# Hidden layer of the late units by sixteen block products for eighteen, and the decay's sigmoid by the hyperbolic tangent

## The chip, the cores and the metric

The kernel runs on one core of one Trainium2 chip. The metric is the device time of the whole kernel in microseconds (us). The engines are named as in the profile: PE (TensorE matmuls), PEld (its weight loads), DVE (VectorE), ACT (ScalarE), POOL (GpSimd), SP (the queue from which most transfers are issued).

## The reference

A gated recurrence (4 batches, 8 heads, 768 steps, head size 48) is followed by a two-layer block with the quick gelu. All data is float32.

```python
f = 1.0 / (1.0 + np.exp(-f_logit))
for t in range(S):
    state = f[:, :, t, :, None] * state + np.einsum('bhd,bhe->bhde', k[:, :, t], v[:, :, t])
    y[:, :, t] = np.einsum('bhd,bhde->bhe', q[:, :, t], state)
x = y.transpose(0, 2, 1, 3).reshape(B * S, H * D)      # 3072 tokens x 384
h = x @ w_in                                           # 384 x 2048
g = h * (1.0 / (1.0 + np.exp(-1.702 * h)))
out = g @ w_out                                        # 2048 x 384
```

## The kernel before, in words

The 3072 tokens are cut into 12 units of 256 tokens (`U`), three per batch. For each unit `attention(n)` computes y in a form without a loop over time: six levels of scores (`level`, `levels`), products of decays made on POOL (`begin_gates`, tile `tot`), states per chunk of 64 tokens (`st`), and y from masked scores and states. `begin_f` turns the gate's logits into the layout of the kernel and takes their sigmoid into tile `F`; for the late units DVE turns (L332) and ACT takes the sigmoid of 128x1024 in place (L337). The last part of a unit writes y through `yT` into `xT` (`to_x`, DMAs from SP), which holds the 384 columns in three thirds of 128 by 256 tokens; the last unit has one token more, since a unit's outputs are shifted by one token.

The two-layer block works on `xT`. `w_in` and `w_out` stay in SBUF. The 2048 hidden columns are 16 blocks of 128 (`ff`). `mlp_h` computes one block of h at a time: three matmuls with 256 moving columns (tokens) into one PSUM bank, and a gelu by ACT into a tile `g` (L785, L789). Units 0 to 2 are done in pieces while weights still arrive (`mlp_block`: `mlp_h` and `mlp_o`). From unit 3 on (`mlp_unit`) all 16 blocks of h are done and then the output by `mlp_o7`, which already uses seven products of half-size blocks for eight: 2x2 blocks of tokens (128) by 192 output columns, with sums of g (`sums_of_a`, `last_sum`, on DVE) and of `w_out` (`sums_of_b`, once) and sums of the results on the way out (`p1` to `p7`, `store`).

PE's order is written out by hand. `merge(n, ...)` emits the attention parts of one unit and puts pieces of the block's work from the list `fill` between them, by a share of columns for each kind of part (`late`); so unit n - 1's h and out products stand between unit n's attention parts. `xT` of unit n - 1 is made at the head of merge n. The other engines' instructions are placed by a scheduler. PSUM has eight banks: four single ones with the tag `mm` that rotate over h, out and turned blocks, two for scores (`sc`) and two for y.

For every fp32 matmul in the code the profile shows two records.

Of the kernel before, what the change touches and what calls it, by code (L numbers as in the profile page):

```python
# [23 lines left out]
def kernel(  # L24
# [37 lines left out]
    P = 128  # L62
# [37 lines left out]
    A = const.tile([P, 2 * NP, 2, HS], F32, name="A")  # L100

    def keep_up(times, columns=384, of=None):

        if times:
            pt = ps.tile([P, columns], F32, tag="mm", name=f"idle_{next(serial)}", bufs=4)
        for _ in range(times):
            lhs, rhs = of or (ident, masks.rearrange("p l f t -> p (l f t)"))
            nc.tensor.matmul(pt, lhsT=lhs, rhs=rhs, start=True, stop=True)  # L108
# [169 lines left out]
    def load_v(n):  # L278


        if n >= NALL:
            return
        b, s0 = n // NU, n % NU * U
        vts[n] = ld.tile([P, 2, DM], F32, tag="vt", name=f"vt_{n}", bufs=2)
        vrs[n] = ld.tile([P, DM], F32, tag="vr", name=f"vr_{n}", bufs=2)
        nc.sync.dma_start(
            out=vts[n][:, 1].rearrange("p (h d) -> p h d", h=H), in_=v[b, :, s0:s0 + HALF, :].rearrange("h p d -> p h d")
        )
        for i in range(4):
            t0 = s0 + U - 32 * (i + 1)  # L290
            nc.sync.dma_start(
                out=vrs[n][32 * i:32 * (i + 1)].rearrange("p (h d) -> p h d", h=H),
                in_=v[b, :, t0:t0 + 32, :].rearrange("h p d -> p h d"),
            )
# [11 lines left out]
    def attention(n):  # L306
# [19 lines left out]
        def turn(j, outs, fn=None):  # L326

            if n >= N_FILL:
                for f in (1, 0):
                    out = outs(f)  # L330
                    at, step = (0, 1) if f else (HALF - 1, -1)
                    nc.vector.transpose(  # L332
                        view(out, at, [[HALF, NP], [step, R4], [R4 * step, 32]]),
                        by_half[:, j, f].rearrange("p a (j d) -> p (a j) d", j=R4)[:, :, :32],
                    )
                if fn:
                    nc.scalar.activation(F, F, fn)  # L337
                return
            for j0 in range(0, R, 4):
                pt = ps.tile([P, 4, P], F32, tag="mm", name=f"t_{n}_{j}_{j0}", bufs=4)  # L340
# [6 lines left out]
                for f in (1, 0):  # L347
                    at, step = (j0, 1) if f else (HALF - 1 - j0, -1)
                    nc.scalar.activation(
                        view(outs(f), at, [[HALF, NP], [R * step, 16], [step, 4]]),  # L350
                        pt.rearrange("p j (a f i) -> p f a i j", a=NP, f=2)[:, 1 - f],
                        fn if fn and n < N_FILL - 1 else AF.Copy,
                    )
            if fn and n == N_FILL - 1:
                nc.scalar.activation(F, F, fn)

        def begin_f():
            turn(0, lambda f: F[:, ORDER.index(f) * SLOT:(ORDER.index(f) + 1) * SLOT], AF.Sigmoid)
            if n >= N_FILL or (n == 1 and 0 == 0):
                load_raw(n + 1, 0)  # L360
# [164 lines left out]
        def turn_k(a0):  # L525
            if a0 == 0:
                new_kn()
            pt = ps.tile([P, 2, 2, P], F32, tag="mm", name=f"tkn_{n}_{a0}", bufs=4)
# [70 lines left out]
        def _():  # L599
# [21 lines left out]
            xT = xTs[n] = mlp.tile([P, NK, width(n)], F32, tag="xT", name=f"xT_{n}", bufs=3)  # L621
            for f in (1, 0):
# [6 lines left out]
            if n == NALL - 1:  # L629

                pl = ps.tile([P, NP], F32, tag="mm", name="y_last", bufs=4)
# [10 lines left out]
                to_x(lambda h: (yl[rows(h), :NK], lambda r, d: yl[r:r + d, NK]), xT[:, :, U:], 1)  # L642
# [48 lines left out]
    def sums_of_a(n, g, b):  # L691

        j = b % 2
        t0, t1 = slice(0, G), slice(G, 2 * G)
        tt = nc.vector.tensor_tensor
        if b < 2:
            g["S", j] = mlp.tile([P, FG, width(n)], F32, tag="g", name=f"S_{n}_{j}", bufs=6)
            tt(g["S", j][:, :, t1], g[j][:, :, t0], g[j][:, :, t1], ALU.subtract)
        else:
            tt(g[j][:, :, t1], g[j][:, :, t1], g[j + 2][:, :, t1], ALU.add)  # L700
            tt(g["S", j][:, :, t0], g[j][:, :, t1], g[j][:, :, t0], ALU.subtract)

    def last_sum(n, g):

        for j in range(2):
            by = slice(0, G)
            nc.vector.tensor_tensor(g[j + 2][:, :, by], g[j + 2][:, :, by], g["S", j][:, :, by], ALU.subtract)

    def mlp_o7(n, g):
        a = lambda i, j: lambda f: g[j * 2 + f // FG][:, f % FG, i * G:(i + 1) * G]  # L710
        s = lambda i: lambda f: g["S", f // FG][:, f % FG, i * G:(i + 1) * G]
        b = lambda i, j: lambda f: quarter(w_out, i, j)[:, f]
        T_ = lambda i: lambda f: T[i][:, f] if i < 4 else T[4](f)
        t = {}

        def out_(tt):
            if "o" not in g:
                g["o"] = mlp.tile([P, U // P, DM], F32, tag="osb", name=f"osb_{n}", bufs=1)
            return g["o"][:, tt]

        def row(name):
            t[name] = mlp.tile([P, HC], F32, tag=name, name=f"{name}_{n}", bufs=1)
            return t[name]

        def p1():
            nc.scalar.copy(row("p1"), t["X"])

        def p4():
            nc.scalar.copy(row("p4"), t["W"])

        def p2():
            nc.scalar.copy(out_(0)[:, :HC], t["X"])
            last_sum(n, g)

        def p6():
            nc.scalar.copy(row("p6"), t["Y"])

        def p5():
            nc.scalar.copy(row("p5"), t["Z"])

        def p7():
            nc.vector.tensor_tensor(row("u3"), t["p1"], t["Y"], ALU.add)
            nc.vector.tensor_tensor(out_(1)[:, :HC], t["u3"], t["p4"], ALU.subtract)
            nc.vector.tensor_tensor(out_(1)[:, HC:], t["u3"], t["p5"], ALU.add)
            store(n, 1, out_(1))

        def p3():
            nc.vector.tensor_tensor(out_(0)[:, HC:], t["p1"], t["Z"], ALU.add)
            nc.vector.tensor_tensor(out_(0)[:, HC:], out_(0)[:, HC:], t["p6"], ALU.add)
            store(n, 0, out_(0))  # L750


        products = (
            ("X", a(0, 0), b(0, 0), p1, True), ("W", a(1, 1), T_(4), p4, True), ("X", a(0, 1), b(1, 0), p2, False),
            ("Y", s(0), T_(2), p6, True), ("Z", a(1, 0), T_(1), p5, True), ("Y", s(1), T_(3), p7, False),
            ("Z", a(0, 1), b(1, 1), p3, False),
        )

        def one(bank, lhs, rhs, done, new, f):
            if new and f == 0:  # L760
                t[bank] = ps.tile([P, HC], F32, tag="mm", name=f"o_{n}_{bank}", bufs=4)
            nc.tensor.matmul(  # L762
                t[bank], lhsT=lhs(f), rhs=rhs(f), start=(new and f == 0), stop=(f == HF - 1), skip_group_check=True,
            )
            if f == HF - 1:
                done()
        return [(HC, lambda p=p, f=f: one(*p, f), 0) for p in products for f in range(HF)]


    xTs = {}  # L770

    def width(n):

        return U + (n == NALL - 1)

    def mlp_h(n, ffs, g, sums=False):
        t = {}

        def one(ff, c):
            if c == 0:  # L780
                if ff % FG == 0:
                    g[ff // FG] = mlp.tile([P, FG, width(n)], F32, tag="g", name=f"g_{n}_{ff}", bufs=6)
                t["ph"] = ps.tile([P, width(n)], F32, tag="mm", name=f"h_{n}_{ff}", bufs=4)
# [4 lines left out]
            if c == NK - 1:  # L788
                nc.scalar.activation(g[ff // FG][:, ff % FG, :], ph, AF.Gelu_apprx_sigmoid)  # L789
                if sums and ff % FG == FG - 1:  # L790
                    sums_of_a(n, g, ff // FG)
                if width(n) > U:

                    by = g[ff // FG][:, ff % FG, U:]
                    if ff == 0:
                        g["last"] = mlp.tile([P, 1, DM], F32, tag="sum", name="sum_last", bufs=3)
                        nc.vector.tensor_scalar(g["last"][:, 0], w_out[:, 0, :], by, None, op0=ALU.mult)
                    else:
                        nc.vector.scalar_tensor_tensor(
                            g["last"][:, 0], w_out[:, ff, :], by, g["last"][:, 0], op0=ALU.mult, op1=ALU.add  # L800
                        )
        return [(NK * U, lambda ff=ff: [one(ff, c) for c in range(NK)], ff // FG * NPC + ff % FG + 1) for ff in ffs]

    def mlp_o(n, ffs, g, done):
# [3 lines left out]
        def one(tt, ff):  # L808
            if ff == ffs[0]:
                t["po"] = ps.tile([P, DM], F32, tag="mm", name=f"o_{n}_{tt}_{ff}", bufs=4)  # L810
# [13 lines left out]
    def mlp_unit(n):  # L824
        g = {}

        def last_token():
            po = ps.tile([P, DM], F32, tag="mm", name="o_last", bufs=4)
# [4 lines left out]
        if width(n) > U:  # L833
            o.insert(3 * HF, (DM, last_token, 0))
        return mlp_h(n, range(NFF), g, True) + o
# [72 lines left out]
    def merge(n, fill, columns, share, pieces=0, hold=0, by=1.0, chores=(), deal=()):  # L908
# [9 lines left out]
        for kind, fn in parts:  # L918
            ready = state["done"]
            fn()  # L920
            for chore in chores[:2]:
                chore()
            chores = chores[2:]
# [27 lines left out]
    UNIT = NFF * NK * U + U // P * NFF * DM  # L951

# [24 lines left out]
    for n in range(3, NALL):  # L977
        fill += mlp_unit(n)
    with nc.allow_non_contiguous_dma("one token"):
        for h in range(2):  # L980
            nc.sync.dma_start(out=q_end[h * HS:h * HS + D], in_=q[B - 1, h::2, S - 1, :].rearrange("a d -> d a"))
    for n in range(4, NALL):
        merge(n, fill, NFF * NK * U + 7 * HF * HC, late, chores=list(sums_of_b()) if n == 4 else ())
# [31 lines left out]
```

## Time and profile before

| | |
|---|---|
| time, median of 3 runs | 628.38 us (627.27 to 629.58) |
| span of the profiled execution | 627.9 us |
| PE, PEld, DVE, ACT, POOL busy | 602.8, 517.5, 385.8, 260.3, 39.9 us |
| h matmuls, L785 | 1152 records, 257.4 us busy |
| gelu of h, L789 | 192, mean 383 ns |
| out products by seven, L762 | 1008 records |
| DVE sums of g, L698, L700, L701, L707 | 18 each, mean 685 to 692 ns |
| POOL products of decays, L383, by size of output: 512, 256, 128 columns | 12 each, mean 1039, 693, 479 ns |
| ACT table loads, L337 and L789 | 9 and 10, 1283 ns each |

In the rows of the profile, a group is a line of the kernel, an engine, an operation, and output and input tiles with their shapes; "x" is the number of records. The mean of a matmul is the time from its start to its end in the pipeline; the next one starts earlier, so the pace is read from starts. Unit 4's h begins at 264 us, and later units follow every 46 us.

### The profile page before, as it was taken

Reading aid. Unit: us, or ns where it says so; the run is one execution under the profiler, and the core shown is the slowest. Engines: PE = TensorE matmul, PEld = TensorE weight load, DVE = VectorE, ACT = ScalarE, POOL = GpSimd, SP = SyncE. Lnnn points to the kernel's source line nnn. Section 1 sums busy time; section 2 is a strip of 40 time slices with the busy share of each in tenths; the row PEclk is TensorE's granted clock in tenths of the full one; section 3 lists DMA queues with packets and bytes.
Section 4 is the critical chain, followed back from the end, with each engine's and each line's share of the span. In section 5 each row is a group of like instructions: output and inputs, shape, how many; then the busy total and the mean of one; then the engine's idle time right before and its main releaser. Section 6 shows DMA issues by size and latency. Waiting matters only on the chain.

```text
span 627.9 us, 17094 instructions
## 1 busy us (share of the span) xinstructions
PE 602.8 (96%) x7314; PEld 517.5 (82%) x7314; DVE 385.8 (61%) x632; ACT 260.3 (41%) x544; POOL 39.9 (6%) x91
## 2 busy tenths in 40 slices
PE   7958999889999999999999999999999999999997
PEld 5647776757678688989989989989989889889896
DVE  1778976575876755677566577656658645521441
ACT  3436543533244534543544454354354353233220
POOL 3010030020001001001001001001001001000000
PEclk9898999989999999999999999999999999999999
DMA  7646675652034444444452342552161121001000
GB/s 171 183 126 165 170 161 158 148 139 76 2 92 99 122 100 105 105 94 110 122 135 60 76 109 73 142 123 68 45 160 33 44 59 27 27 1 27 26 1 25
DMA packets 83308, 58.20 MB, mean 93 GB/s; under 512 B 33633, under 2 KB 75265, under 8 KB 83233
## 3 DMA queue, kind: packets, MB, share of 16 engines
q1 hardware_dynamic: 82192, 55.55, 35.4%
q10 hardware_dynamic: 1041, 1.57, 1.0%
q8 instruction: 57, 0.93, 0.7%
q14 instruction: 18, 0.15, 0.1%
HBM read 43.98 MB, written 8.39 MB: 83 GB/s over the span
## 4 chain that ended last, share of the span: by engine, by line
PE 87%; DVE 6%; ACT 3%; DMA 2%; issue 1%; SPq 1%; ACTq 0%; DVEq 0%
PE h L785 38%; PE o_X L762 8%; PE o_Y L762 8%; PE o L811 8%; PE o_Z L762 7%; PE sc L392 6%; PE o_W L762 4%; PE t L344 3%; PE y L616 2%; PE sc L576 2%; PE y L488 1%; PE idle L108 1%; DVE a L221 1%; DMA xT<-yT 1%; ACT yT L627 1%
## 5 line engine op out<-in xcount | busy, mean ns | idle before, releaser
L785 PE MATMUL h<-xT,w_in 128*128 128x256 f32 (+1 forms) x1152 | 257.4, 381 | 2.4 <-ACT g L789 1.9
L785 PEld LDWEIGHTS h<-xT,w_in 128*128 128x128 f32 x1152 | 216.4, 190 | 34.2 <-ACT g L789 2.1
L789 ACT ACTIVATE g<-h 128x256 f32<-128x256 f32 (+1 forms) x192 | 72.0, 383 | 156.8 <-PE h L785 156.5
L477 DVE TENSOR_TENSOR X<-X,tot 128x1024 f32<-128x1024 f32 x45 | 55.1, 1224 | 62.6 <-PE sc L392 49.4
L448 ACT COPY Kc<-X 128x512 f32<-128x512 f32 x72 | 48.0, 666 | 83.4 <-DVE X L477 51.3
L811 PE MATMUL o<-w_out,g 128*128 128x384 f32 x192 | 67.5, 501 | 3.0 <-DVE w_out L222 3.0
L811 PEld LDWEIGHTS o<-w_out,g 128*128 128x128 f32 x192 | 36.2, 194 | 26.0 <-DVE w_out L222 3.6
L762 PE MATMUL o_X<-w_out,g 128*128 128x192 f32 x288 | 52.6, 331 | 0.0
L762 PE MATMUL o_Y<-T,S 128*128 128x192 f32 x288 | 51.9, 329 | 0.0
L441 DVE COPY_PREDICATED A<-masks,sc 128x256 f32<-128x256 uint32 (+1 forms) x108 | 50.9, 534 | 0.1
L762 PEld LDWEIGHTS o_Y<-T,S 128*128 128x128 f32 x288 | 46.9, 190 | 1.5 <-issue 0.7
L762 PEld LDWEIGHTS o_X<-w_out,g 128*128 128x128 f32 x288 | 46.7, 190 | 1.0
L383 POOL TENSOR_TENSOR tot<-F 128x512 f32<-128x512 f32 x12 | 12.5, 1039 | 478.2 <-DVE st L594 429.3
L392 PE MATMUL sc<-X,Kc 48*64 48x64 f32 x1440 | 31.1, 224 | 10.7 <-ACT Kc L448 9.6
L392 PEld LDWEIGHTS sc<-X,Kc 48*64 48x64 f32 x1440 | 26.4, 138 | 18.0 <-ACT Kc L448 11.4
L332 DVE STREAM_TRANSPOSE X<-raw 128x512 f32<-128x512 f32 x36 | 37.9, 1101 | 2.9 <-PE y L616 2.8
L700 DVE TENSOR_TENSOR g<-g,g 128x512 f32<-128x512 f32 x18 | 12.5, 692 | 40.4 <-ACT g L789 40.4
L627 ACT COPY yT<-y 48x256 f32<-48x256 f32 x92 | 33.7, 366 | 7.8 <-PE y L616 5.3
L473 DVE TENSOR_TENSOR X<-X,tot 128x512 f32<-128x512 f32 x30 | 20.3, 688 | 13.1 <-PE sc L392 11.0
L383 POOL TENSOR_TENSOR tot<-tot 128x256 f32<-128x256 f32 (+4 forms) x60 | 24.6, 410 | 4.7
L762 PE MATMUL o_W<-T,g 128*128 128x192 f32 x144 | 24.9, 326 | 0.0
L762 PE MATMUL o_Z<-w_out,g 128*128 128x192 f32 x144 | 24.9, 326 | 0.0
(92 smaller groups left out, 629.1 us busy)
## 6 DMA issues: line engine op xcount, KB each, us to landing
bits<-in_moe_w_out_dram SPq DMA_DIRECT2D x8, 768.0 KB, 5.0
raw<-in_f_logit_dram SPq DMA_DIRECT2D x48, 96.0 KB, 2.3
raw<-in_k_dram SPq DMA_DIRECT2D x48, 96.0 KB, 2.3
raw<-in_q_dram SPq DMA_DIRECT2D x44, 96.0 KB, 2.3
bits<-in_moe_w_in_dram SPq DMA_DIRECT2D x7, 576.0 KB, 6.2
k_tok<-z SPq DMA_DIRECT2D x56, 64.0 KB, 1.8
kt<-k_tok SPq DMA_DIRECT2D x14, 256.0 KB, 2.8
out_dram<-osb SPq DMA_DIRECT2D x18, 192.0 KB, 1.8
```

Of the source, the lines that this page charges most:

```text
L332: nc.vector.transpose(view(out, at, [[HALF, NP], [step, R4], [R4 * step, 32]]), by_half[:, j, f].rearrange("p a (j d) -> p (a j) d", j=R4) ...
L383: nc.gpsimd.tensor_tensor(tn, t2[:, :, 0], t2[:, :, 1], ALU.mult)
L392: nc.tensor.matmul(t["sc"][g * HS:(g + 1) * HS, h, a, s, :], lhsT=t["Kc", l][rows(h), x:x + HS], rhs=rhs(h, a, g), start=True, stop=True,)
L441: nc.vector.copy_predicated(out=view(A, at, dims), mask=mask.bitcast(U32), data=got)
L448: nc.scalar.copy(c.rearrange("p (n two m) -> p n two m", two=2, m=m), view(X, KF * SLOT, [[2 * m, SLOT // (2 * m)], [(KR - KF) * SLOT + m, ...
L473: nc.vector.tensor_tensor(x, x, y, ALU.mult)
L477: nc.vector.tensor_tensor(x, x, y, ALU.mult)
L627: copy(view(yT[rows(h)], at, [[U, NP], [step, HS]]), py[columns(h, g), g, :, f, :])
L762: nc.tensor.matmul(t[bank], lhsT=lhs(f), rhs=rhs(f), start=(new and f == 0), stop=(f == HF - 1), skip_group_check=True,)
L785: nc.tensor.matmul(ph, lhsT=w_in[:, c, ff * P:(ff + 1) * P], rhs=xTs[n][:, c, :], start=(c == 0), stop=(c == NK - 1))
L789: nc.scalar.activation(g[ff // FG][:, ff % FG, :], ph, AF.Gelu_apprx_sigmoid)
L811: nc.tensor.matmul(t["po"], lhsT=g[ff // FG][:, ff % FG, tt * P:(tt + 1) * P], rhs=w_out[:, ff, :], start=(ff == ffs[0]), stop=(ff == ffs[ ...
```

## The change

For units 4 to 11 a new `mlp_h16` takes the place of `mlp_h`. The first twelve blocks of the hidden columns are seen as three rows of four blocks, `w_in` as a matrix of 3 by 3 parts (row of hidden columns by a third of the 384 inputs), and the tokens as two halves, so h of the three rows is a 3x3 by 3x2 product of blocks. Done block by block it is 18 block products; here it is 16, each of a sum of `w_in` parts and a sum of x parts, each over four blocks of hidden columns with 128 moving columns. The products are put in four chains; in a chain each product adds to what stands in the bank, and most running sums on the way are one summand of an output and are read out before the chain goes on. An output needs one or two such summands: the first is copied by ACT, the second added by DVE, then ACT takes the gelu in place; one output is complete at once and goes through the gelu from the bank. The last four blocks of hidden columns are computed as before, one at a time, between the chains' products, in the order `SEQUENCE`.

The sums of `w_in` are made once: those in new tiles by `sums_of_w` (POOL and DVE, as chores of merge 4, now three to a part), those that overwrite `w_in` by `sums_in_place` in the middle of unit 3's out products. The sums of x (`sums_of_x`) are eleven POOL instructions per unit, right after `xT` is made. `g` becomes three tiles of eight blocks for six of four; `xT` and two tiles of sums share three buffers; the four single PSUM banks are named one by one (`bank`, `lanes`). `sums_of_a` comes after all of h. Two of the intermediate rows of the out part are summed in the output tile. In the last unit (one token more) the halves have 129 columns, the chains run over two blocks at a time, and the row sums of the last token come after h. The decay's sigmoid becomes 0.5 + 0.5 tanh(x/2) from unit 1 on, with the affine part on POOL (`half_up`).

```diff
@@ turn, begin_f @@
-                        fn if fn and n < N_FILL - 1 else AF.Copy,
+                        (AF.Tanh if n else AF.Sigmoid) if fn else AF.Copy, scale=0.5 if fn and n else 1.0,
...
+        def half_up():
+            nc.gpsimd.tensor_scalar(F, F, 0.5, 0.5, op0=ALU.mult, op1=ALU.add)
+        def sigmoid():
+            nc.scalar.activation(F, F, AF.Tanh, scale=0.5)
+            half_up()
@@ load_v, turn_k @@
-        vrs[n] = ld.tile([P, DM], F32, tag="vr", name=f"vr_{n}", bufs=2)
+        vrs[n] = ld.tile([P, DM], F32, tag="vr", name=f"vr_{n}", bufs=1)
...
+            if n < N_FILL + 1:
+                pt = bank([P, 2, 2, P], f"tkn_{n}_{a0}")
+            else:
+                pt = ps.tile([P, 2, 2, P], F32, tag="sc", name=f"tkn_{n}_{a0}")
@@ end of attention @@
+            if width(n) > U:
+                nc.gpsimd.memset(xT[:, :, U + 1:], 0.0)
...
+            if n > N_FILL:
+                sums_of_x(n)
@@ sums_of_a, last_sum @@
+        S = g["S"] = g_tile(f"S_{n}", width(n))
+        fs = [slice(f, f + HF // 2) for f in (0, HF // 2)]
+        for f in fs:
+            tt(S[:, f, t1], g[0][:, f, t0], g[0][:, f, t1], ALU.subtract)
+        for f in fs:
+            tt(g[0][:, f, t1], g[0][:, f, t1], g[1][:, f, t1], ALU.add)
+        for f in fs:
+            tt(S[:, f, t0], g[0][:, f, t1], g[0][:, f, t0], ALU.subtract)
@@ mlp_o7 @@
         def p2():
-            nc.scalar.copy(out_(0)[:, :HC], t["X"])
+            plus(0, left, "X")
             last_sum(n, g)
...
         def p7():
-            nc.vector.tensor_tensor(row("u3"), t["p1"], t["Y"], ALU.add)
-            nc.vector.tensor_tensor(out_(1)[:, :HC], t["u3"], t["p4"], ALU.subtract)
-            nc.vector.tensor_tensor(out_(1)[:, HC:], t["u3"], t["p5"], ALU.add)
-            store(n, 1, out_(1))
+            plus(1, left, "Y")
+            plus(1, right, "Y")
+            store(n, 1, g["o"][:, 1])
@@ new @@
+    CHAINS = (
+        (("D5", "b21", 3), ("N6", "E12", 2), ("C4", "E4", 4), ("N3", "E15", 0), ("a00", "E6", 1), ("N4", "E10", 5)),
+        (("N5", "b21", None), ("N1", "b11", 1), ("D11", "E11", None), ("D8", "E3", 0)),
+        (("a22", "E3", None), ("D9", "E9", 4), ("N7", "b10", None), ("N2", "E14", 2)),
+        (("a10", "E0", None), ("D2", "b11", 3)),
+    )
+    NEGATIVE = 0, 2, 5
+    SEQUENCE = "0 1 2 0 1 2 p 0 1 2 p 0 1 2 p 0 3 3 p 0".split()
+    LANE = {"0": 0, "1": 1, "2": 2, "3": 1, "p": 3}
...
+        by("E4", "b10", sub, "b00")
+        by("E12", "E4", add, "b21")
+        by("E3", "b20", add, "b21")
+        by("E10", "b01", add, "b21")
+        by("E0", "E10", sub, "b11")
+        by("E15", "E12", add, "b11")
+        by("E6", "E10", sub, "E15")
+        by("E9", "b00", sub, "b21")
+        by("E11", "b10", add, "b11")
+        by("E11", "E11", add, "E3")
+        by("E14", "E4", sub, "b20")
...
+            for t in range(group.start, group.stop):
+                nc.tensor.matmul(
+                    ph[:, t - group.start], lhsT=WA[a][:, t * P:(t + 1) * P], rhs=E[n][b],
+                    start=(i == 0 and t == group.start), stop=(i == len(CHAINS[chain]) - 1), skip_group_check=True,
+                )
+            if out is None:
+                return
...
+            if out == CHAINS[0][-1][2]:
+                nc.scalar.activation(to, ph, AF.Gelu_apprx_sigmoid, scale=scale)
+            elif (group.start, out) not in begun:
+                begun.add((group.start, out))
+                nc.scalar.copy(to, ph)
+            else:
+                nc.vector.tensor_tensor(to, to, ph, ALU.add)
+                nc.scalar.activation(to, to, AF.Gelu_apprx_sigmoid, scale=scale)
...
+        def end():
+            sums_of_a(n, g)
+            if width(n) > U:
+                sum_last(g)
@@ mlp_unit @@
-            o.insert(3 * HF, (DM, last_token, 0))
-        return mlp_h(n, range(NFF), g, True) + o
+            o.insert(6 * HF, (DM, last_token, 0))
+        if n > N_FILL:
+            return mlp_h16(n, g) + o
...
+        return mlp_h(n, range(NFF), by_block) + [(0, end, 0)] + o[:4 * HF] + [(0, sums_in_place, 0)] + o[4 * HF:]
@@ merges @@
+    H16 = 16 * FG * G + FG * NK * U
...
-        merge(n, fill, NFF * NK * U + 7 * HF * HC, late, chores=list(sums_of_b()) if n == 4 else ())
+        merge(n, fill, (H16 if n > N_FILL + 1 else NFF * NK * U) + 7 * HF * HC, late, chores=w_sums if n == 4 else [])
```

## The prediction

> **What bounds the kernel now.** I read the page's busy shares and its clock row first, then the busy times by stage, then the waits of the stage that changes, and last the timeline, because the mean duration of a matmul is a latency and not its pace.
>
> ```profile
> PE 602.8 (96%) x7314; PEld 517.5 (82%) x7314; DVE 385.8 (61%) x632; ACT 260.3 (41%) x544; POOL 39.9 (6%) x91
> ...
> PEclk9898999989999999999999999999999999999999
> ...
> 286.20:332.20 46.00, 46.00 (x593) 42.01 (x592) 29.26 (x46) 21.15 (x44) 2.81 (x6) 1.00 0.44 109
> 332.20:378.10 45.90, 45.90 (x597) 42.12 (x597) 29.71 (x47) 20.97 (x43) 2.81 (x6) 1.00 0.35 84
> 378.10:423.90 45.80, 45.80 (x594) 42.05 (x593) 29.61 (x47) 21.02 (x43) 2.81 (x6) 1.00 0.47 114
> ```
>
> The last three lines are one unit each (stretch, length, then busy PE, PEld, DVE, ACT, POOL). From unit 4 on PE is busy all of it at full clock, with DVE at 29.5 us, ACT at 21 and POOL at 2.8 of 45.8 us. PE's largest waits between 264 and 605 us are these, in total, times and longest:
>
> ```profile
> PEld sc L392 <- issue: 3.7, 13, 0.3
> PEld y L488 <- issue: 2.3, 7, 0.3
> PEld y L616 <- issue: 1.3, 6, 0.2
> PEld o_Y L762 <- ACT p L736: 0.3, 1, 0.3
> PEld y L616 <- DVE F L332: 0.2, 1, 0.2
> ```
>
> Only the last two, 0.5 us, are for another engine: the order written out for PE is the bound, and a column taken off PE is worth its pace. The pace, from start to start:
>
> ```profile
> 380.02 2.87 PE L762 MATMUL o_X<-w_out,g 128*128 128x192 f32 x16
> 382.72 2.76 PE L762 MATMUL o_W<-T,g 128*128 128x192 f32 x16
> 385.32 1.46 PE L762 MATMUL o_X<-w_out,g 128*128 128x192 f32 x8
> ...
> 550.99 0.60 PE L532 MATMUL tkn<-ident,X 128*128 128x128 f32 x4
> 551.19 0.38 ACT L789 ACTIVATE g<-h 128x256 f32<-128x256 f32 x1 [0.91 <-PE h L785]
> 551.32 0.30 PEld L785 LDWEIGHTS h<-xT,w_in 128*128 128x128 f32 x2
> 551.43 0.38 PE L785 MATMUL h<-xT,w_in 128*128 128x256 f32 x1
> ```
>
> The 16 o_W records take 385.32 - 382.72 = 2.60 us, 162.5 ns each at 192 columns. By the same reading of the trace's starts, h records of 256 columns come every 216 ns (217 to 218 over a unit), o records of 384 every 322, and the four 128-column records at 550.99 every 0.11 us. Every fp32 matmul in the code is two records: 16 blocks by 3 make 48 matmuls, and a unit has 96 h records.
>
> **What the skill says.** (1) The Trainium skill, "TensorE: Matmul & The Clock Gate", "Back-to-back issue gap", gives N/2.4 + 2.5 ns warm. The trace agrees if a record streams each column twice: 2 x 192/2.4 + 2.5 = 162.5, 2 x 256/2.4 + 2.5 = 215.8. For 128 columns that is an estimate of 109.2 ns. (2) The same page, "LDWEIGHTS (loading the stationary operand)", has P/1.2 ns: 107 for 128 weight columns, so weight load and matmul would be just level. Trace: weight loads of 64 columns last 136 ns, of 128 columns 190, so 54 ns per 64, which agrees; and the first two loads of the filler at 39.61 us start 0.11 us apart. The same section on the gap also says that a stream of N=128 pairs ran at 81 ns where the formula has 56; doubled that would be 162. No run here shows such a stream of plain 128-column matmuls; the four at 550.99 are transposes, whose weight loads last 141 ns and not 190. (3) "ScalarE: Activation LUTs", "What ACT_TABLE_LOAD costs": 1283 ns; the trace has exactly 1283, twice per late unit (L337 and L789). It lists tanh beside sigmoid; whether the set of the gelu used here holds it, it doesn't say. (4) "GPSIMD Engine Reference", "1. Specifications": POOL shares its SBUF interface with DVE. The trace agrees: the five small POOL products of a unit take 2.09 us alone and 3.46 and 4.02 us where DVE is converting weights.
>
> **The change, part by part.**
>
> *h of units 4 to 11.* It removes 12 blocks x 3 = 36 matmuls of 256 columns, 72 records: 72 x 216 = 15.55 us. It adds 16 products x 4 blocks = 64 matmuls of 128 columns, 128 records: 128 x 109.2 = 13.98 us. Four plain blocks stay. That is 1.57 us per unit; unit 11 (258 for 257 columns, halves of 129 at 110 ns) gets 1.5. Eight units: -12.5 us. Bounds of the pace: 107 (the load alone) and 162.
>
> *Evictions of h.* 12 ACT gelus of 383 ns (4.6 us) become 5 ACT copies of a 128x512 bank (L533: 591 ns), 6 gelus of the same size (about 650) and 5 DVE adds (L700: 692): ACT 6.9 us, DVE +3.5. ACT comes to about 23 and DVE to 33 of 44 us: neither becomes the bound. What counts is that a chain's bank is read between its products, and PE may not write on. Reading costs about 0.2 us to start (the gelus start 0.2 us after a block's end), 0.6 to 0.7 for the instruction and about 0.1 back: 1.0 us. A product is 8 x 109 = 0.87 us, a plain block 6 x 216 = 1.3 us, so the hand-written sequence puts 1.7 us ahead of chain 0's second product and 3.0 us ahead of each later one. Alone, nothing waits. But both engines take their queues in order, and DVE is full from 359.9 to 370 us with transposes of 1.1 us in the middle of h: an add that stands behind two of them is late by some tenths. I take 0.2 us per unit (bounds 0 and 1.5): +1.6 us.
>
> *Sums of x.* 11 POOL sums of 128x128. Nearest row: L383 with 128x128, 479 ns; 11 make 5.3 us. They start when xT has landed: its last DMA is issued until 395.06 us and lands in 1.8 to 2.6 us, so about 397.2; h begins at 401.79 in the old trace. Since merge 5 still emits the old number of columns for a shorter unit, the stock of out products ahead of h shrinks by 1,024 columns, 1.7 us, to about 400.1. The first sum needed, the third, is there at 398.7, wanted by the third product at 401.8; the eighth at 401.1, wanted after 405. Hidden, with 3 us to spare. xT, two sum tiles and g now turn over each unit, but what they overwrite was last read by h or out products that PE had done by then. Cost 0, up to 4 us per unit if the price is three times as high.
>
> *Sums of h and the out part.* The eight DVE sums of 0.69 us stay eight, but six now come after h: 4.2 us from about 1 us behind its end, while PE first has 2.0 us of attention and three products of 2.6. Hidden; the states (L594, L595) behind them on DVE have 4 us before the y products want them. One DVE op and one copy fewer per unit. 0.
>
> *Weight sums.* 9 POOL and 2 DVE instructions of about 1.04 us in merge 4, DVE at 61% there: hidden. The seven in-place sums (5 DVE, 2 POOL, some 0.7 to 1.0 us each) come in unit 3's out part, with 8 to 9 us before unit 4's h; the first product wants one of them at once. +0.7 us (0 to 2.5).
>
> *Decay by the tangent.* It takes away up to 19 table loads of ACT and adds a POOL pass over 128x1024 for units 1 on, about 1.7 us by the slope of L383's rows. In a late unit F is ready at 388.5 and first used at 370 of the next unit, 27 us on: nothing either way. In units 1 and 2 a table load or POOL pass might show: 0 (-1 to +1.5).
>
> *Queues.* The v staging buffer goes from two to one; its load is issued after the shuffle that reads it, so SP does not wait. k turned through the score bank: only unit 11, 2.6 us apart, 0.
>
> *The last unit.* It is too wide for one bank, so it runs in two groups of two blocks: a product is 0.44 us and a chain's bank has 0.9 us to be read in about 0.8. The 16 row sums for the last token (some 10 us on DVE) and six sums now start after h, and are wanted after the sixth out product, 15.6 us on: just in time. +1.0 (0 to 4). At the very end one DVE add of 0.35 less.
>
> Sum: -12.5 + 1.6 + 0.7 + 1.0 - 0.35 = -9.6 us. The profiled span is 627.9, so 618.3; the three runs shown are 627.27 to 629.58, median 628.38, and from that median I say 618.8.
>
> **Rivals.**
>
> *Chain banks wait for engines in order.* As above, but 1.2 us per unit in place of 0.2: about 626. For it: DVE's dense 10 us, and that the adds are emitted behind those transposes. Against: 3.0 us between reads, and four of the old sums leave that stretch.
>
> *Weight load sets the pace at 128 columns (slower).* If a load can't run wholly under the matmul before it, a record costs 158 (190 less the 32 by which transposes' loads outlast their spacing) and not 109: 128 x 49 = 6.3 us per unit, 50 in all, hence 669. It decides from 121 ns on, where the 1.57 us are gone. For it: 190 ns of load, 81 for 56 in the skill. Against: loads 0.11 us apart at 39.61; and the first 192-column record behind small matmuls costs only 0.1 us extra (o_X at 380.02: 2.70 for 2.60), which is all of an exposed load.
>
> *x sums come late (slower).* At three times 479 ns, from DVE's share of the port, the eighth sum comes 4 us late; seven units, about 28 us, 647. It decides from about 0.95 us per sum. Against: even the slowest stretch of POOL in the trace is only twice its normal time.
>
> *The table stays loaded twice* if tanh isn't in gelu's set: ACT keeps 2.6 us per unit, still under the bound; same time as the forecast.
>
> **How the numbers follow.** A measurement of this kernel can tell about 0.5%, 3.1 us. Forecast 0.63, all faster, its own range 614 to 623. Chain banks 0.18: 0.08 faster, 0.07 same, 0.03 slower. Weight load 0.08 and x sums 0.06, slower. Anything else 0.05: 0.01 faster, 0.02 same, 0.02 slower. Together faster 0.72, same 0.09, slower 0.19. The range 613 to 630 holds the forecast and most of the chain-bank case, and leaves out the two slower rivals and the tails.
>
> **What would show it.** Right: h records of 128 columns about 109 ns apart, units of about 44.3 us, PE waits for h of some tenths, POOL's sums done before the products want them, ACT table loads down to two or three. Wrong: PEld waits at h for ACT, DVE or POOL of over 1 us per unit, or a pace over 121 ns.

## The result and the profile after

The changed kernel takes 620.25 us (median of 4 runs, 620.18 to 621.44); the kernel before, measured beside it, 627.83 us (4 runs, 626.52 to 629.58). The ratio is 0.9862, 95% interval 0.9834 to 0.9889. Measured again beside other runs of before (629.27 us), the changed kernel took 619.02 us, ratio 0.9832 (0.9809 to 0.9856). The profiled span is 618.5 us, against 627.9. By the medians the gain is 7.6 us in the first measurement and 10.3 in the second; the 9.4 us of the two profiles lie between.

The busy shares on the page after:

```profile
PE 593.3 (96%) x7762; PEld 525.3 (85%) x7762; DVE 421.5 (68%) x675; ACT 252.0 (41%) x519; POOL 121.1 (20%) x202
```

PE has 448 more matmul records and is busy 9.5 us less: many more, but shorter ones. POOL's work has tripled, DVE has 36 us more, and yet the span fell by what PE lost. One late unit of the changed kernel (stretch, length, then busy PE, PEld, DVE, ACT, POOL, each with its instructions; clock, DMA share, GB/s):

```profile
398.40:442.98 44.58, 44.58 (x650) 43.01 (x649) 30.41 (x48) 20.10 (x40) 9.43 (x17) 1.00 0.42 102
```

A unit lasts 44.58 us where it lasted 45.83, PE is busy in all of it, and DVE, ACT and POOL stay far below. PEld, though, went from 42.1 to 43.0 us: read that as the first sign that weight loads now have little room. The waits of PE at h between 264 and 605 us (total, times, longest) show what the chains cost:

```profile
PEld h L883 <- ACT g L894: 0.7, 1, 0.7
...
PE h L883 <- ACT g L894: 0.5, 1, 0.5
```

In eight units of chains, h waits for another engine once, and the two lines for L894 are that one stall seen from the weight load and from the matmul. It is in the last unit, between its two groups. The timeline of PE there (start, length, and in brackets the idle time before and what ended it):

```profile
585.00 0.61 PE L883 MATMUL h<-E,N 128*128 128x129 f32 x4
586.09 0.71 PE L883 MATMUL h<-xT,w_in 128*128 128x129 f32 x4 [0.48 <-ACT g L894]
```

The product at 585.00 ends chain 0 of the first group, and the next product of PE's order opens chain 0 of the second group in the same bank: the gelu must read it out in between. 1.09 us pass from start to start, where four 129-column records take 0.45.

In a full unit the chain banks are never waited for. PE in the first part of a unit's h, with the order of `SEQUENCE` (its fifth and sixth product, of chains 1 and 2, and the first plain block):

```profile
447.84 1.06 PE L883 MATMUL h<-xT,N 128*128 128x128 f32 x8
448.73 1.06 PE L883 MATMUL h<-E,w_in 128*128 128x128 f32 x8
449.62 1.46 PE L905 MATMUL h_p<-xT,w_in 128*128 128x256 f32 x6
```

And POOL in the same unit, making the sums of x for it, with one instruction of DVE in that time:

```profile
437.85 1.93 POOL L856 TENSOR_TENSOR E<-xT 128x128 f32<-128x128 f32 x2 [7.57 <-DMA xT<-yT]
...
443.21 0.45 POOL L856 TENSOR_TENSOR E<-xT 128x128 f32<-128x128 f32 x1
...
438.24 1.22 DVE L491 TENSOR_TENSOR X<-X,tot 128x1024 f32<-128x1024 f32 x1 [2.31 <-PE sc L406]
```

From start to start a product of eight records takes 0.89 us: 111.7 ns a record. Nine of POOL's eleven sums take 0.45 us. The other two take 1.52 us (the second of the first row) and 1.43: each begins while DVE makes a product of 128x1024 (L491, the first of two is shown) and ends 0.3 us after it. E9, the eighth sum in the code, is ready at 443.66; the product that reads it starts at 448.73.

ACT's table loads in the changed kernel (busy us, mean ns, idle time before):

```profile
L118 ACT ACT_TABLE_LOAD x1 | 1.3, 1283 | 0.7 <-PEq L1193 0.7
L984 ACT ACT_TABLE_LOAD x1 | 1.3, 1283 | 0.0
```

There were 20, now there are 2: with tanh, the decay and the gelu share one table. More of the gain hangs on this than the prediction allowed, as the experiments show.

By stages, the 9.4 us of span come from these places:

| stage | before | after | difference |
|---|---|---|---|
| start to unit 4's h | 264.05 | 264.63 | +0.58 |
| unit 4's h to unit 11's h, seven units | 320.09 | 311.06 | -9.03 |
| unit 11's h | 20.86 | 20.26 | -0.60 |
| the rest, to the end | | | -0.35 |

The first row holds two things: unit 3's h begins 1.27 us later, and from there to unit 4's h it takes 0.69 us less (45.84 for 46.53), where a wait of 0.5 us for ACT that the kernel before has (L576 for `kn`) is gone. The seven units are 7 x 1.26 us and 0.25 more, since the first of them took 46.08 before.

### The profile page after: what moved, and what is told of

Its sections match the earlier page's. It is cut to its first block, busy times and chain, and to the rows that moved or that the text cites. A ratio compares the mean times of both kernels' runs of the same rounds, so it can differ in the third digit from the quotient of the medians.

```text
span 618.5 us, 18187 instructions
## 1 busy us (share of the span) xinstructions
PE 593.3 (96%) x7762; PEld 525.3 (85%) x7762; DVE 421.5 (68%) x675; ACT 252.0 (41%) x519; POOL 121.1 (20%) x202
## 4 chain that ended last, share of the span: by engine, by line
PE 88%; DVE 7%; ACT 2%; issue 1%; DMA 1%; ACTq 0%; SPq 0%; DVEq 0%
PE h L883 19%; PE o_Y L785 12%; PE h L980 12%; PE o L994 9%; PE o_Z L785 8%; PE h_p L905 7%; PE sc L406 6%; PE o_X L785 4%; PE o_W L785 4%; PE t L350 2%; PE y L633 2%; PE y L502 2%; PE sc L593 1%; ACT yT L646 1%; DVE X L487 1%
## 5 line engine op out<-in xcount | busy, mean ns | idle before, releaser
L491 DVE TENSOR_TENSOR X<-X,tot 128x1024 f32<-128x1024 f32 x45 | 57.1, 1270 | 56.2 <-PE sc L406 50.3
L980 PE MATMUL h<-xT,w_in 128*128 128x256 f32 x384 | 88.5, 386 | 2.4 <-ACT g L984 1.8
L980 PEld LDWEIGHTS h<-xT,w_in 128*128 128x128 f32 x384 | 72.3, 192 | 14.8 <-ACT g L984 2.0
L883 PE MATMUL h<-E,w_in 128*128 128x128 f32 (+1 forms) x448 | 58.1, 276 | 0.0
L397 POOL TENSOR_TENSOR tot<-F 128x512 f32<-128x512 f32 x12 | 12.5, 1039 | 229.7 <-DVE st L611 224.1
L883 PEld LDWEIGHTS h<-E,w_in 128*128 128x128 f32 x448 | 54.7, 192 | 1.2
L455 DVE COPY_PREDICATED A<-masks,sc 128x256 f32<-128x256 uint32 (+1 forms) x108 | 51.9, 531 | 0.1
L899 DVE TENSOR_TENSOR g<-g,h 128x512 f32<-128x512 f32 (+1 forms) x45 | 27.8, 626 | 33.7 <-PE h L883 33.4
L984 ACT ACTIVATE g<-h 128x256 f32<-128x256 f32 x64 | 24.0, 383 | 60.7 <-PE h L980 60.3
L905 PE MATMUL h_p<-xT,w_in 128*128 128x256 f32 (+1 forms) x192 | 46.8, 380 | 0.0
L897 ACT COPY g<-h 128x512 f32<-128x512 f32 (+1 forms) x45 | 24.3, 539 | 44.7 <-PE h L883 44.3
L856 POOL TENSOR_TENSOR E<-xT 128x128 f32<-128x128 f32 (+1 forms) x40 | 26.6, 678 | 68.3 <-DMA xT<-yT 36.0
L905 PEld LDWEIGHTS h_p<-xT,w_in 128*128 128x128 f32 x192 | 34.0, 191 | 3.3
```

Source lines behind the costliest of these rows:

```text
L455: nc.vector.copy_predicated(out=view(A, at, dims), mask=mask.bitcast(U32), data=got)
L491: nc.vector.tensor_tensor(x, x, y, ALU.mult)
L883: nc.tensor.matmul(ph[:, t - group.start], lhsT=WA[a][:, t * P:(t + 1) * P], rhs=E[n][b], start=(i == 0 and t == group.start), stop=(i == ...
L899: nc.vector.tensor_tensor(to, to, ph, ALU.add)
L905: nc.tensor.matmul(ph, lhsT=w_in[:, c, (ROWS * FG + f) * P:(ROWS * FG + f + 1) * P], rhs=xTs[n][:, c, :], start=(c == 0), stop=(c == NK - 1),)
L980: nc.tensor.matmul(ph, lhsT=w_in[:, c, ff * P:(ff + 1) * P], rhs=xTs[n][:, c, :], start=(c == 0), stop=(c == NK - 1))
```

## The experiments

**The pace alone (e_pace).** What set the new pace, 111.7 ns for the 109.2 of the stream formula? This kernel only loads one weight tile and streams matmuls of many sizes (the computation of the reference is left out whole).

```diff
+    for n, (cols, weights) in enumerate(((64, 128), (96, 128), (112, 128), (120, 128), (128, 128), (136, 128), (160, 128), (192, 128), (64, 64), (96, 64), (128, 64), (128, 96))):
+        stream(cols, weights, 48, (n + 1) % 2)
```

> This kernel leaves the whole computation out: it only streams fp32 matmuls, 48 (96 records) of each kind back to back, each with weights of its own, over 64 to 192 moving columns, and writes a meaningless output. If the weight load sets the pace of the 128-column products (111.6 ns in the changed kernel, where the formula has 109.2), records with 128 weight columns come every 111 to 112 ns at 64, 96, 112, 120 and 128 moving columns alike, 115.8 at 136, 135.8 at 160 and 162.5 at 192; with 64 weight columns at 64 moving columns about 56 to 58. If it is a fixed extra cost of a record, the pace falls with the columns: about 58, 85, 98, 105 and 112 ns at 64, 96, 112, 120 and 128.

The groups by shape (input x weight columns, then output with moving columns, records | busy us, mean ns). Busy over 96 records is 1 to 2 ns above the pace, since it takes in the end of the last record; the paces below are from starts:

```profile
L67 PE MATMUL b<-W 128*128 128x136 f32 x96 | 11.3, 279 | 0.0
L67 PE MATMUL b<-W 128*128 128x96 f32 x96 | 10.9, 276 | 0.0
...
L67 PE MATMUL b<-W 128*128 128x128 f32 x96 | 10.9, 275 | 0.0
...
L67 PE MATMUL b<-W 128*64 128x128 f32 x96 | 10.6, 273 | 0.0
...
L67 PE MATMUL b<-W 128*64 128x64 f32 x96 | 5.8, 222 | 0.0
```

All have 128 inputs. With 128 weight columns the starts are 111.7 to 112.0 ns apart for 96, 112, 120 and 128 moving columns alike, and the median is 112 also at 64; 136 columns take 115.9 and 192 take 162.5, as the stream formula says. With 64 weight columns the same 128 moving columns take 109.2, and 64 take 58.8. So there is a floor of 111.7 ns that depends on the width of the weights and not on the columns streamed; that points to the weight load. At 128 columns it lies only 2.5 ns over the stream. The Trainium skill, "TensorE: Matmul & The Clock Gate", "LDWEIGHTS (loading the stationary operand)", gives P/1.2, 107 ns; measured it is 111.7. The slowdown that the page's section "Back-to-back issue gap" has at N = 128, 81 ns for the formula's 56, isn't seen here at fp32.

**The chains without their interleaving (e_chain_row).** Does the hand-written order hide the reads of the banks, or are they free? Chain 0 runs in a row.

```diff
-    SEQUENCE = "0 1 2 0 1 2 p 0 1 2 p 0 1 2 p 0 3 3 p 0".split()
+    SEQUENCE = "0 0 0 0 0 0 1 2 1 2 p 1 2 p 1 2 p 3 3 p".split()
```

> The changed kernel with chain 0's six products in a row and the other chains and plain blocks after them. If the interleaving is what hides the reads of the banks, each of the five reads between chain 0's products shows as a PE wait: 0.2 us to start, 0.59 for the copy, about 0.1 back, so 0.9 us; 4.5 us in each of seven wide units and 10 reads of 0.7 in the last: 39 us more, about 659. If PE goes on while the bank is read, or the reads are much shorter, the time stays at 620.

One run: 662.51 us, span 660.7, 42.2 over the changed kernel; units of 48.5 to 50.1 us. Its PE timeline in one unit:

```profile
413.23 1.05 PE L883 MATMUL h<-xT,w_in 128*128 128x128 f32 x8
415.05 1.13 PE L883 MATMUL h<-E,N 128*128 128x128 f32 x8 [0.77 <-ACT g L897]
```

The second product of the chain starts 1.82 us after the first, and not 0.89: one read of a 128x512 bank costs PE 0.92 us if nothing else is put there. PE's matmuls wait 20.7 us in all, 28 times, for such copies between 264 and 605 us. So the estimate of 1.0 us for a read was right, and the order hides it whole: the shortest gap that a read gets, two other products (1.79 us), is twice what it needs.

**The sigmoid as it was (e_sigmoid).** The whole change but its tangent: the table is loaded twice per unit again.

```diff
-                        (AF.Tanh if n else AF.Sigmoid) if fn else AF.Copy, scale=0.5 if fn and n else 1.0,
+                        AF.Sigmoid if fn and n < N_FILL - 1 else AF.Copy,
...
-            nc.scalar.activation(F, F, AF.Tanh, scale=0.5)
-            half_up()
+            nc.scalar.activation(F, F, AF.Sigmoid)
```

> The changed kernel with the sigmoid as before, no tangent and no POOL pass. If the table loads are hidden behind ACT's slack (20 of 44.6 us busy), late units stay at 44.58 us and only the first 140 us can get shorter, by up to 1.5 us: 618.5 to 620.5. If the chains' reads need a free ACT, the load of 1.28 us at the head of h delays the first copies and PE waits show at h: 0.3 to 1 us per late unit, 622 to 628.

627.26 us (median of 12 runs), ratio to before 0.9974 (0.9956 to 0.9991), span 625.2. I had expected the loads to hide; they do not, and without the tangent nearly the whole gain is gone. Five successive late units last 44.76, 45.79, 45.03, 45.87 and 45.05 us: 3.6 us more than five of 44.58; from unit 4's h to unit 11's it is 315.19 us for 311.06. Unit 4's h starts at 267.27, 2.6 us later. ACT is busy only 22 to 23 of 45 us all the while, so it is not how much ACT has to do, but how late one of its reads comes. One place shows it. ACT's timeline in this kernel, with the table load and, further on, the copy that reads the bank of Y:

```profile
342.35 1.28 ACT L368 ACT_TABLE_LOAD   x1 [3.71 <-DVE F L338]
...
350.87 0.31 ACT L758 COPY osb<-o_Y 128x192 f32<-128x192 f32 x1
```

PE's timeline in this kernel, where it writes Y again:

```profile
351.23 0.59 PE L784 MATMUL o_Y<-T,S 128*128 128x192 f32 x2 [0.37 <-ACT osb L758]
```

The same copy on ACT's timeline in the changed kernel, with the tangent:

```profile
346.09 0.31 ACT L759 COPY osb<-o_Y 128x192 f32<-128x192 f32 x1
```

And there PE's next write of Y:

```profile
347.32 0.49 PE L785 MATMUL o_Y<-T,S 128*128 128x192 f32 x2
```

With the tangent the bank Y is read until 346.40 and written again at 347.32: 0.92 us of margin. With the sigmoid the copies of yT, Kc and Qc behind the table load all move by about its length against PE (yT starts 4.77 us later in the one trace than in the other, PE's stream at that place 3.38), the read of Y stands behind them in ACT's queue, and it comes 1.40 us later against PE: the margin is gone and PE waits. From 288 to 575 us the weight loads wait 2.6 us in five places for this copy, and 1.0 us in two for a gelu of a plain block (L908), behind the other table load of the unit, which falls on the first gelu of h. Together that is about the loss of the late units. It does not come at the chains' reads, where I had looked for it, but mostly in the out part.

Was this read new? No: the kernel before reads Y at the same place (L736) and writes it again one product later, with the table load ahead of it. Lines from its timelines of DVE, PE and ACT (F turned, the product in between, the read of Y, the next write):

```profile
338.24 2.06 DVE L332 STREAM_TRANSPOSE F<-raw 128x512 f32<-128x512 f32 x2 [0.85 <-POOL tot L383]
346.87 2.76 PE L762 MATMUL o_Z<-T,g 128*128 128x192 f32 x16
348.84 0.31 ACT L736 COPY p<-o_Y 128x192 f32<-128x192 f32 x1
349.47 0.81 PE L762 MATMUL o_Y<-T,S 128*128 128x192 f32 x4
```

And the first two of them in e_sigmoid:

```profile
340.22 2.05 DVE L338 STREAM_TRANSPOSE F<-raw 128x512 f32<-128x512 f32 x2 [0.83 <-POOL tot L396]
348.10 2.76 PE L784 MATMUL o_Z<-T,g 128*128 128x192 f32 x16
```

In the kernel before the read ended 0.31 us ahead of the write here, and 0.05 to 0.32 us in all six such places from 257 to 487 us: the load was hidden, but only just. DVE turns F, which the load waits for, 8.63 us ahead of the product there, and 7.88 us ahead of it in e_sigmoid. The six sums of g that now come after h stand before it: the first copy of the states on DVE starts 0.07 us after PE's part of them in the kernel before, and 1.14 us after it here, straight behind those sums. A margin of 0.31 us less 0.75 is a wait. This is read from the traces; no run moves the sums of g alone.

The late start is one place too. Around unit 3's decay PE waits 4.50 us for a gelu, with two table loads ahead of that gelu on ACT, where it waits 1.80 us in the changed kernel, and then the granted clock is 0.72 for 5.6 us (1.00 in the changed kernel). The stretch of PE around it takes 13.97 us; in all ten profiles with the tangent in unit 3 and the same products there it takes 9.74 to 9.76.

**The tangent alone (e_tanh_alone).** Only the decay of the kernel before is changed.

```diff
-                    nc.scalar.activation(F, F, fn)
+                    nc.scalar.activation(F, F, AF.Tanh, scale=0.5)
+                    half_up()
...
-                        fn if fn and n < N_FILL - 1 else AF.Copy,
+                        (AF.Tanh if n else AF.Sigmoid) if fn else AF.Copy, scale=0.5 if fn and n else 1.0,
```

> The kernel before with the decay by the tangent and nothing else. If the table loads only hurt together with the new products, whose banks and rows must be read at shorter notice, late units stay at 45.8 us and the time is that of before, 627 to 630. If the loads held PE up in the kernel before as well, or ACT's order changes for the better, the late units get shorter by the 0.3 to 0.8 us a unit that the changed kernel loses without the tangent: 622 to 625.

627.10 us (20 runs), ratio 0.9970 (0.9958 to 0.9983). Its late units last 45.82 to 45.84 us, as before but for the first, which took 46.08 there. The rest of the profile's 2.1 us is gained ahead of unit 3's h, where profiles of one code differ by up to 2.9 us (below), so its place is not known; over the runs the medians are 2.2 us apart. The read of Y and the next write, from ACT's and PE's timelines:

```profile
346.13 0.31 ACT L740 COPY p<-o_Y 128x192 f32<-128x192 f32 x1
...
347.47 0.81 PE L766 MATMUL o_Y<-T,S 128*128 128x192 f32 x4
```

The margin is 1.03 us for 0.31. So in the kernel before, the table loads of the late units were hidden, as the prediction said, but with little to spare; in the changed one they would not be. Alone, the two halves of the change give 0.9974 and 0.9970, which multiplies to 0.9944; together they give 0.9862, or 0.9832 in the second measurement. The rest, 0.8 to 1.1%, exists only for both.

**The new h from unit 8 on (e_from8).** Is the gain one per unit, or once? (The sums of x, the in-place sums of `w_in` and the columns of the merges move with it.)

```diff
-        if n > N_FILL:
+        if n > 7:
             return mlp_h16(n, g) + o
```

> The changed kernel with the sixteen products only from unit 8 on; units 4 to 7 take the eighteen. If the gain is the difference of matmul paces in each unit (72 x 216 less 128 x 111.6 = 1.27 us), units 4 to 7 take 45.8 us and the others 44.6, and the span is 4 x 1.27 = 5 us over that of the changed kernel, 623.5. If the gain came once, from the order or the start, it is nearer to 618 or 628.

625.17 us (10 runs), ratio 0.9931 (0.9909 to 0.9952). One unit of each kind:

```profile
378.99:424.83 45.84, 45.84 (x594) 42.09 (x593) 33.87 (x51) 18.38 (x40) 6.85 (x9) 1.00 0.44 110
469.41:513.99 44.58, 44.58 (x649) 43.01 (x648) 33.20 (x52) 20.30 (x39) 10.97 (x18) 1.00 0.20 52
```

1.26 us per unit, in the very unit that has the chains.

**The sums of x twice and three times (e_xsums_2, e_xsums_3).** The rival that would have made the kernel slower: from what price of a sum on does h wait?

```diff
-            nc.gpsimd.tensor_tensor(e[out], e[x], e[y], op)
+            for _ in range(1 if out == x else 3):
+                nc.gpsimd.tensor_tensor(e[out], e[x], e[y], op)
```

> The changed kernel with ten of the eleven POOL sums of x done twice, into the same place. In the profile the eighth sum ends 5.1 us before the product that reads it and the sums take 0.6 us each; doubled, the eighth is about 0.3 us early or 0.8 late: 620 to 626. If POOL's share of the port gets worse under the longer run, more.

> As the run with two, three times each. If the sums are the rival that I named, hidden by about 5 us and not more, the eighth comes 5 to 6.5 us late in each of seven units: PE waits for POOL at h, 655 to 665. If PE's order hides them further (other products go on), no more than 630.

Twice: 621.70 us in one run, span 619.9, late units still 44.58 us and no wait for POOL. Three times: 651.09 us, span 649.3, and units of 47.3 to 49.8 us. PE in the latter:

```profile
413.31 1.06 PE L884 MATMUL h<-xT,N 128*128 128x128 f32 x8
417.01 2.07 PE L884 MATMUL h<-E,w_in 128*128 128x128 f32 x8 [2.64 <-POOL E L857]
```

The product that waits is the one that reads the eighth sum, as the rival had it; in all h waits 20.9 us for POOL, and the run is a little under the 655 to 665 expected. The rival's mechanism is real, and its threshold lies between two and three times the sums as they are: in the trace after, the eighth sum is 5.1 us ahead of its use.

**The sigmoid for the first units only (e_sig_first, e_sig_first_5).** Units 1 and 2 keep the sigmoid; the tangent, with POOL's pass over `F`, comes from unit 3 on.

```diff
-                        (AF.Tanh if n else AF.Sigmoid) if fn else AF.Copy, scale=0.5 if fn and n else 1.0,
+                        AF.Sigmoid if fn and n < N_FILL - 1 else AF.Copy,
...
-            if fn and n:
-                half_up()
+            if fn and n == N_FILL - 1:
+                nc.scalar.activation(F, F, AF.Sigmoid)
```

> The changed kernel with the sigmoid as before in units 0 to 2 and the tangent from unit 3 on. If the table load and the POOL passes of units 1 and 2 are what made the start 0.6 us later (unit 4's h at 264.63 for 264.05), this takes 0.5 to 1.5 us off the stretch before unit 4: 619 to 620, late units unchanged. If that was chance of the clock in the first 40 us, no change.

> Sigmoid in units 0 to 2, tangent from 3 on, again and with more rounds. If what it gained is the order of ACT and POOL in units 1 and 2, it is again 2.5 to 3 us ahead of the changed kernel at unit 3 (about 238.3 us) and in the time, ratio about 0.982. If it was chance, no difference from the changed kernel.

618.66 us (4 runs), ratio 0.9835 (0.9811 to 0.9859), and in a second measurement 618.24, ratio 0.9813 (0.9790 to 0.9836). Beside that second one the changed kernel itself was run again:

> The changed kernel itself again, beside the three below. Expected as before: ratio 0.986, span 618 to 620; the attention product of unit 3 (y from A) starts between 240.9 and 242.4 us, as in the runs that share its start.

It gave 619.02 us, ratio 0.9832. The mark ahead of unit 3 (its first y product) came at 239.51 us, not in the range I had given: in seven profiles with the same code up to there it lies between 239.51 and 242.37, so the start differs by up to 2.9 us by chance. Much of that goes with the granted clock: its mean from 10 to 140 us is 0.96 in the earliest of the seven and 0.93 in the latest. With the sigmoid first, three profiles have 238.26 to 239.57; beside profiles with the same mean clock (0.95 or 0.96) they are 0.6 to 1.3 us ahead. Of that, 0.7 us is in one place: the same products of PE, from 61.93 to 68.99 us in the trace after, take 7.06 us there and 6.32 with the sigmoid first (61.04 to 67.36). The 2.5 to 3 us that the second run was to show again did not come. Times are lower, intervals overlap: in the time the gain stays open.

**The order of the last unit (e_last), and both (e_both).** The one stall that is left is moved: in the first group of the last unit a plain block stands between chain 0's end and its next beginning.

```diff
+            last_first = len(groups) > 1 and group is groups[0]
+            for chain in ("0 1 2 0 1 2 p 0 1 2 0 1 2 0 3 3 0 p".split() if last_first else SEQUENCE):
```

> The changed kernel with one plain block of the last unit moved behind the first group's last product of chain 0, so that its bank is read while PE does the plain block. If the 0.65 and 0.1 us at 585.0 and 586.1 us of the changed kernel are that read, the last unit's h gets 0.75 us shorter, 19.5 for 20.26; too little for the time to show. If the wait moves to the next product, no change.

> Both: sigmoid in units 0 to 2 and the moved plain block in the last. The two lie at opposite ends of the kernel, so they add: 2.6 and 0.75 us, span 615 to 615.5, ratio about 0.981, below both the kernel before and the changed one.

The last unit's h takes 19.52 us for 20.26, and the place now reads:

```profile
583.21 0.61 PE L883 MATMUL h<-E,N 128*128 128x129 f32 x4
583.65 1.47 PE L905 MATMUL h_p<-xT,w_in 128*128 128x258 f32 x6
584.96 0.61 PE L883 MATMUL h<-xT,w_in 128*128 128x129 f32 x4
```

No wait stands there any more, which is the 0.74 us. In the time that is too little to see: 618.91 us, ratio 0.9825 (0.9804 to 0.9847). With the sigmoid for the first units as well: 618.21 us, ratio 0.9820 (0.9794 to 0.9847), the lowest median of all, but not to be told from the changed kernel; the span of 616.4 us is over the 615 to 615.5 expected, since the 2.6 us at the start were mostly chance.

## Why the prediction was right, and where not

The direction and the bound (the order written out for PE) were right, and so was the size: -9.6 us of span forecast and -9.4 found, 618.8 us forecast and 620.25 and 619.02 measured. The terms were less so. The pace gave 2.3 us less than forecast, and the waits of the chains and the in-place sums, 2.3 us together, did not come. That the sum came out so near is luck.

*Pace of the 128-column records.* Forecast 109.2 ns, measured 111.7 in the kernel and by itself; in eight units the h matmuls give about 10.2 us (7 x 1.27, with 72 x 216 = 15.55 less 128 x 111.6 = 14.28, and 1.3 in the last), not 12.5; e_from8 measures 1.26 per unit. The step took the stream formula and held the load, by the skill 107, to be just under it; the load is just over it. This is the rival "weight load sets the pace" at a fraction of its size: 111.7, well under the 121 from which that rival would decide.

*Waits at the chain banks.* Forecast +1.6, measured 0. The argument that alone nothing waits was right (e_chain_row gives the price of a read, 0.92 us, and the order gives it twice that); the tenths added for engines in order did not come. DVE's adds are never what PE waits for. ACT is busy 20 us per unit and not about 23: that sum left in the table loads that the change takes away.

*In-place sums at unit 4.* Forecast +0.7, measured 0: from unit 3's h to unit 4's it takes 45.84 us, with no PE wait for DVE or POOL, and unit 4 takes 44.58 us like the others.

*Last unit.* Forecast +1.0, measured one stall of about 0.75, at the bank between the groups. The sums for the last token, half of the reason, show in no wait of PE.

*Sums of x.* Hidden, as forecast, with 5.1 us to spare for the 3 forecast. The mean sum takes 0.63 us, under the rival's 0.95. A sum that meets one of DVE's large products does take three times 479 ns, but only two in eleven do; e_xsums_3 shows that the rival's mechanism was sound.

*Tangent.* Forecast "nothing either way", since F is needed only 27 us later. This is the step that failed. Its reasoning looked at the use of what the sigmoid makes, and not at what stands behind its table load in ACT's queue: the copy that reads Y before it is written again. That read had 0.05 to 0.32 us of margin in the kernel before, and the one wait it caused (`o_Y L762 <- ACT p L736`, 0.3 us) stands in the prediction's own list. A second term that was put at nothing takes the margin away: the six sums of g after h are hidden for the states, as it said, but DVE turns F 0.75 us later behind them. For the kernel before, the statement nearly holds (e_tanh_alone: late units unchanged but for 0.25 us in one). For the kernel with the other changes in, it is 4.1 us from unit 4's h to unit 11's, and 6.7 us over the whole span. The rival that the table stays loaded twice was given the forecast's time; e_sigmoid shows that it would have been 627.

*Start.* Forecast 0 (-1 to +1.5), found +0.58, inside what profiles with the same code differ by. The tangent costs 0.7 us in one place of units 1 and 2, as e_sig_first shows; up to 1.3 us are possible.

What stays open besides: whether the order of the sums of g alone takes away the margin of Y's read, and where the 2.2 us of e_tanh_alone are gained.

## What to carry to other kernels

Price an instruction on an engine with much spare time by what is queued behind it and by how soon others want that. A table load that is hidden by 0.3 us can decide once what it waits for comes 0.75 us later, so two edits may be worth something only together; a wait of a few tenths in the profile before is a sign that a margin is used up. Chains that add up in a bank and are read on the way cost PE nothing here with 1.79 us of other matmuls in between, for a read of 0.92 us; look for the place where the order wraps around, here between the last unit's groups. Fewer block products with fewer moving columns pay by the pace of the narrower record, so measure that pace by itself before anything else.

## What the runs showed of the hardware

An fp32 record with 128 weight columns takes at least 111.7 ns, flat from 64 to 128 moving columns (e_pace); with 64 weight columns it takes 58.8 ns for 64 and 82.5 for 96. From 136 columns on (115.9 ns, and 162.5 at 192) the time grows by 0.83 ns a column, so the two meet at about 131 columns, by estimate: cutting blocks narrower than that shortens a record with full-width weights no further.

Tanh and the gelu used here are in one table: 2 loads in the whole kernel. The Trainium skill, "ScalarE: Activation LUTs", "What ACT_TABLE_LOAD costs", has 1283 ns for a load; the trace has the same in every one.

A small POOL sum can be held up by one DVE instruction as a whole. Of the 77 sums of 128x128 in units 4 to 10, 63 take 0.45 to 0.47 us. The other 14, two in each unit, take 1.43 to 1.52, and each of them begins inside DVE's product of two tiles of 128x1024 (L491) and ends 0.3 us after it. Beside DVE's predicated copies (L455) and its additions from a bank (L746) the sums keep their 0.45 us.
